# Where the big on-chip buffer begins: 192 bytes ahead of KV in a decode kernel that streams 170 MB

## The chip, the core and the metric

The kernel runs on one core of a Trainium2 chip. The metric is the device time of one execution in microseconds (us); before the change it is 402.7 us, the median of three runs (402.51 to 402.73).

## What is computed

One token goes through two branches whose results are added to it: an attention block with a cache of 65,536 positions, and a small mixer MLP. All data are bf16.

```python
def _A_ref(x, k_cache, v_cache, wq, wo):      # x [1,1,1024], k/v_cache [1,4,65536,128]
    q = heads(x @ wq)                          # 32 query heads of 128, 8 to a KV head
    scores = einsum("bhqd,bhkd->bhqk", q, k) * (128 ** -0.5)
    o = einsum("bhqk,bhkd->bhqd", softmax(scores), v)
    return merge(o) @ wo
def _B_ref(x, w1, w2, w3, w4):
    h = gelu(layernorm(x) @ w1)                # then a shift along the one position
    x1 = x + shifted(h) @ w2
    return x1 + gelu(layernorm(x1) @ w3) @ w4
xn = layernorm(A_x)
return A_x + _A_ref(xn, ...) + _B_ref(xn, ...)
```

With a sequence of length one the shift leaves only zeros, so the product with w2 is a product with zeros; the kernel still loads w2. Every cached key and value and every weight is read exactly once: 67 MB of keys, 67 MB of values and 36 MB of weights.

## The kernel before

**The buffer.** On-chip memory is laid out by the calls of `sb(...)` (L204), one tensor after another in the order of the calls, each rounded up to a multiple of 32 bytes of a partition. The last of them is `KV` (L257): 98,304 bf16 elements, 196,608 bytes in each of 128 partitions. In the program of before it begins at byte 31,552 of a partition, which is 123 x 256 + 64. All big transfers land in KV: keys in two slots of 32 KB a partition (`KOFF`, L258), values in two slots of 64 KB (`VOFF`), and the weights in the same slots before the first and after the last of the keys and values. `EPI` (L259) is a piece of the first value slot that holds small operands near the end. All offsets inside KV at which a transfer begins (L322, L333, L341, L621 to L627, L650, L651) are multiples of 256 bytes, so what KV's own first byte leaves after division by 256 is what every row of a transfer leaves.

**The transfers.** All of them but that of x are issued by SyncE (SP), from one queue. `issue_k(m)` (L325) loads 4 MB of keys: 128 rows, one to a partition, of 32 KB each. `issue_v(j)` (L335) loads 8 MB of values: 128 rows of 64 KB. wq and wo have rows of 64 KB, w3 of 56 KB, w4 comes in three pieces with rows of 32, 20 and 4 KB, w1 and w2 have rows of 16 KB (`load_rows`, L316, and `load_at`, L579). The 128 rows of a transfer are divided among the core's 16 DMA engines, 8 to each.

**The order.** wq goes first, then K0, V0, K1 (L323, L343 to L345). In the main loop (L584) step n handles 8,192 positions of one KV head; 32 steps in all. A key block serves two steps and a value block four. A slot is reloaded as soon as its last reader is done: `issue_k` after each odd step (L617), `issue_v` after each fourth (L619). So the queue receives K, K, V, K, K, V and so on: 16 key blocks and 8 value blocks, then w1, w2, w3 (L621 to L624), wo and w4 (L626, L627, L657).

**A step.** VectorE (DVE) transposes the keys of the slot in place, as 32-bit words, in four instructions (`Ttr`, L493); TensorE (PE) forms scores from them (`QK`, L503); VectorE takes maxima (L510); ScalarE (ACT) takes the exponential (L531); TensorE and VectorE transpose the result (L539, L541); TensorE multiplies with the values (`PV`, L549); ScalarE copies the product out (L557) and GpSimd (POOL) adds it to the running sum (L560, L562). After the loop come the products with w1, w2, w3, wo and w4 (L464, L665, L452), a cast (L699) and the transfer of the output (L700). The last weights to land are pieces of w4, read at L452.

Of the kernel before, what the change touches and what calls it, by code (L numbers as in the profile page):

```python
# [6 lines left out]
BF = mybir.dt.bfloat16  # L7
# [152 lines left out]
def _dma(q, chan, fn, reads=(), writes=(), partial=False):  # L160
    _deps(q, reads, writes)
    chan.n += 1
    ev = q.dma(fn, chan.sem, 16 * chan.n)
    _done(ev, reads, writes, partial)
    return ev


def bass_parallel_sum__gqa_block_cached__mixer_s_mlp__decode_kernel(
# [13 lines left out]
    P = 128  # L182
# [18 lines left out]
    with ExitStack() as es:  # L201
        E = es.enter_context

        def sb(name, shape, dt):  # L204
            return E(nc.sbuf_tensor(name, shape, dt))
# [48 lines left out]
        acc = sb("acc", [P, KT_D], F32)  # L254
        g_bf = sb("g_bf", [P, KT_D], BF)
        gh_bf = sb("gh_bf", [P, KT_F], BF)
        KV = sb("KV", [P, 98304], BF)  # L257
        KOFF, VOFF = (0, 16384), (32768, 65536)  # L258
        EPI = KV[:, 61440:65536].bitcast(F32)  # L259
        Dmat_f, Pmat_f = EPI[:, 1024:1152], EPI[:, 1152:1280]  # L260
# [29 lines left out]
        def chan(name):  # L290
            if name not in chans:
                chans[name] = _DmaChan(sem("d_" + name))
            return chans[name]
# [22 lines left out]
        def load_rows(dst, bufs, ch, w, r0, nrow):  # L316
            src = w.rearrange("(p r) n -> p (r n)", p=P)
            ncol = w.shape[1]
            _dma(q_sp, chan(ch), lambda e: e.dma_start(out=dst, in_=src[:, r0 * ncol:(r0 + nrow) * ncol]), writes=bufs)

        _dma(q_act, chan("x"), lambda e: e.dma_start(out=x_bf[:, :], in_=A_x[0, 0, :].rearrange("(p j) -> p j", p=P)), writes=[b_x])
        wq_sb = KV[:, VOFF[1]:VOFF[1] + 8 * HQD]  # L322
        load_rows(wq_sb, [b_V[1]], "wq", A_wq, 0, 8)  # L323

        def issue_k(m):  # L325
# [6 lines left out]
            sl = m % 2  # L332
            _dma(q_sp, chan("k%d" % sl), lambda e: e.dma_start(out=KV[:, KOFF[sl]:KOFF[sl] + 16384], in_=src), writes=b_K[sl] + b_T[sl])  # L333

        def issue_v(j):  # L335
# [4 lines left out]
            sl = j % 2  # L340
            _dma(q_sp, chan("v%d" % sl), lambda e: e.dma_start(out=KV[:, VOFF[sl]:VOFF[sl] + 32768], in_=src), writes=[b_V[sl]])  # L341

# [136 lines left out]

        KV32 = KV[:].bitcast(F32)  # L480
        kstep = KV[:].ap[0][0]
        pT_bf = pT_f[:].bitcast(BF).rearrange("p (q r two) -> p q r two", q=16, two=2)
# [253 lines left out]
```

## Time and profile before

| | before |
|---|---|
| median of three runs | 402.7 us |
| the profiled execution | 402.08 us |
| its span in the profile | 400.8 us, so 1.28 us lie around it |
| queue q1 (all big transfers) | 4,616 packets, 169.87 MB, 98.4% of 16 engines' span |
| mean rate over the span | 424 GB/s |
| VectorE, TensorE, GpSimd, ScalarE busy | 58%, 44%, 23%, 12% |
| granted TensorE clock, mean | 0.613 |

The profile is one execution. A busy share is the time in which an engine had an instruction, divided by the span; the DMA's share is the mean of the 16 DMA engines. The trace also holds a record of each DMA packet, with its queue, size, start and duration; here a packet is one row of a transfer (4 KB to 64 KB in one partition) or a 4-byte write that reports an engine's share of a transfer as done. A transfer counts as landed when all 16 engines have reported.

### The profile page before, as it was taken

The numbers are of one execution on the slowest core, as the hardware profiler recorded it, in microseconds if no ns is written. First come the engines' busy times: TensorE is split into PE (matmuls) and PEld (weight loads), VectorE is DVE, ScalarE is ACT, GpSimd is POOL, SyncE is SP. The second block draws the span as 40 slices with busy tenths as digits, with TensorE's granted clock in tenths as the row PEclk, the third lists the DMA queues.
The fourth block names the chain that finished last, engine by engine and source line by source line (L and its number), as shares of the span: only waits on it lengthen the run. The fifth ranks groups of instructions, "written<-read, shape, count | busy, mean of one in ns | idle before, by whom it ended". The sixth has DMA issues, their size and how long they took to land.

```text
span 400.8 us, 4663 instructions
## 1 busy us (share of the span) xinstructions
PE 175.5 (44%) x1504; PEld 54.0 (13%) x1504; DVE 232.5 (58%) x399; ACT 48.6 (12%) x132; POOL 91.5 (23%) x173
## 2 busy tenths in 40 slices
PE   0044244446254525443644464155426443454484
PEld 0022111111011101110111111011101110122132
DVE  0024756883688288738864886487657756643400
ACT  1000010211021101110111020111111120110000
POOL 6000013232135302230253021314332222250000
PEclk9997555655556656665555556656555555565888
DMA  9989999999999999999999998999999989999995
GB/s 392 445 366 471 414 419 419 491 395 422 461 420 422 422 451 464 392 419 458 432 419 419 484 438 386 422 461 438 405 432 484 432 379 425 482 414 413 437 410 210
DMA packets 4768, 169.98 MB, mean 424 GB/s; under 512 B 660, under 2 KB 664, under 8 KB 792
## 3 DMA queue, kind: packets, MB, share of 16 engines
q1 hardware_dynamic: 4616, 169.87, 98.4%
q8 instruction: 5, 0.08, 0.1%
q10 hardware_dynamic: 144, 0.00, 0.0%
q14 instruction: 3, 0.02, 0.0%
HBM read 169.87 MB, written 0.00 MB: 424 GB/s over the span
## 4 chain that ended last, share of the span: by engine, by line
DMA 57%; DVE 18%; PE 13%; issue 10%; ACT 1%; another core or an unknown queue 0%; DVEq 0%; POOL 0%; ACTq 0%; SPq 0%; POOLq 0%
DMA KV<-in_A_k_cache_dram 42%; DVE KV L493 13%; DMA KV<-in_B_w_dram 10%; PE S_ps L503 9%; DMA x_bf<-in_A_x_dram 6%; DVE mrow L510 2%; PE PT_ps L539 2%; PE OT_ps L549 1%; PE MM_ps L464 1%; ACT p_sb L531 1%; DVE pT_f L541 1%; PE MB_ps L516 1%; PE OUT_ps L452 0%; DVE Rm L511 0%; DVE Bst L520 0%
## 5 line engine op out<-in xcount | busy, mean ns | idle before, releaser
L493 DVE STREAM_TRANSPOSE KV<-KV 128x1024 f32<-128x1024 f32 x128 | 149.5, 1211 | 23.1 <-DMA KV<-in_A_k_cache_dram 23.1
L503 PE MATMUL S_ps<-KV,Ycur 128*32 128x512 bf16 x512 | 60.1, 617 | 83.5 <-DVE KV L493 83.2
L562 POOL TENSOR_TENSOR O_acc<-O_acc,tmpO 128x513 f32<-128x513 f32 x32 | 40.8, 1274 | 122.6 <-ACT tmpO L557 122.6
L549 PE MATMUL OT_ps<-KV,pT_f 128*32 128x512 bf16 x512 | 58.7, 609 | 19.5 <-DVE pT_f L541 18.7
L510 DVE TENSOR_REDUCE mrow<-S_ps 128x1 f32<-128x512 f32 x32 | 22.1, 691 | 39.6 <-PE S_ps L503 39.6
L531 ACT ACTIVATE p_sb<-S_ps,brun 128x512 bf16<-128x512 f32 x32 | 21.9, 686 | 136.3 <-DVE brun L529 119.5
L539 PE MATMUL PT_ps<-p_sb,permR 128*128 128x512 bf16 x32 | 17.6, 550 | 45.0 <-ACT p_sb L531 45.0
L557 ACT ACTIVATE tmpO<-OT_ps 128x512 f32<-128x512 f32 x32 | 19.2, 599 | 139.1 <-PE OT_ps L549 80.2
L503 PEld LDWEIGHTS S_ps<-KV,Ycur 128*32 128x32 bf16 x512 | 14.4, 125 | 124.4 <-DVE KV L493 95.4
L541 DVE STREAM_TRANSPOSE pT_f<-PT_ps 128x512 f32<-128x512 f32 x32 | 22.8, 713 | 13.3 <-PE PT_ps L539 12.3
L559 POOL TENSOR_TENSOR spare<-ff 128x1 f32<-128x1 f32 x32 | 6.2, 193 | 101.6 <-ACT ff L535 99.7
L549 PEld LDWEIGHTS OT_ps<-KV,pT_f 128*32 128x32 bf16 x512 | 15.7, 130 | 50.8 <-DVE pT_f L541 29.1
L560 POOL TENSOR_SCALAR O_acc<-O_acc,ff 128x514 f32<-128x514 f32 x32 | 22.4, 701 | 0.2 <-issue 0.2
L516 PE MATMUL MB_ps<-Rm,Lmat 128*128 128x16 bf16 x32 | 6.1, 192 | 25.5 <-DVE Rm L511 25.5
L520 DVE TENSOR_REDUCE Bst<-MB_ps 128x1 f32<-128x16 f32 x32 | 5.6, 174 | 14.2 <-PE MB_ps L516 14.2
L381 PE MATMUL MM_ps<-ln_s,ones_f 128*128 128x1 f32 x6 | 1.8, 362 | 27.1 <-DVE ln_s L380 27.1
L377 DVE CAST xT<-x_bf 128x8 f32<-128x8 bf16 x1 | 0.2, 172 | 21.4 <-DMA x_bf<-in_A_x_dram 21.4
L665 PE MATMUL S_ps<-KV,o_bf 128*1 128x512 bf16 x64 | 8.6, 437 | 5.6 <-DMA KV<-in_A_wo_dram 5.6
L516 PEld LDWEIGHTS MB_ps<-Rm,Lmat 128*128 128x128 bf16 x32 | 3.3, 102 | 53.3 <-DVE Rm L511 53.3
L393 POOL TENSOR_TENSOR ln_s<-ln_s,neghalf 128x1 f32<-128x1 f32 x3 | 1.7, 558 | 37.2 <-DVE ln_s L391 37.2
L539 PEld LDWEIGHTS PT_ps<-p_sb,permR 128*128 128x128 bf16 x32 | 3.2, 102 | 47.8 <-ACT p_sb L531 47.8
L691 DVE COPY KV<-S_ps 64x512 f32<-64x512 f32 x1 | 0.7, 682 | 11.5 <-PE S_ps L665 11.5
(112 smaller groups left out, 120.7 us busy)
## 6 DMA issues: line engine op xcount, KB each, us to landing
KV<-in_A_k_cache_dram SPq DMA_DIRECT2D x16, 4096.0 KB, 23.7
KV<-in_B_w_dram SPq DMA_DIRECT2D x1, 7168.0 KB, 33.2
KV<-in_B_w_dram SPq DMA_DIRECT2D x2, 2048.0 KB, 14.5
KV<-in_B_w_dram SPq DMA_DIRECT2D x1, 4096.0 KB, 35.4
KV<-in_B_w_dram SPq DMA_DIRECT2D x1, 2560.0 KB, 39.1
KV<-in_B_w_dram SPq DMA_DIRECT2D x1, 512.0 KB, 40.0
KV<-in_A_v_cache_dram SPq DMA_DIRECT2D x8, 36.2
x_bf<-in_A_x_dram ACTq DMA_DIRECT2D x1, 2.0 KB, 22.1
```

Source lines behind the costliest of these rows:

```text
L493: ev = q_dve.op(lambda e, c=c: e.transpose(out=KV32[:, c:c + 1024], in_=KV32[:, c:c + 1024]))
L503: fns.append(lambda e, we=we, cm=cm, mv=mv: e.matmul(S_ps[32 * cm:32 * cm + 32, :], Ycur[:, we, :, :].rearrange("p a g -> p (a g)"), mv, s ...
L510: _op(q_dve, lambda e: e.reduce_max(mrow[:, m:m + 1], S_ps[:, :], axis=AX.X), reads=[b_S], writes=[b_mrow[m]])
L516: _op(q_pe, lambda e: e.matmul(MB_ps[:, 0:16], Lmat[:, :], Rm[:, m, :], start=True, stop=True), reads=[b_R[m], b_const], writes=[b_MB])
L531: _op(q_act, lambda e: e.activation(p_sb[:, m, :], S_ps[:, :], ACTF.Exp, bias=brun[:, m:m + 1], scale=SCALE, accum_out=tmpO[:, cL:cL + 1]) ...
L539: _op(q_pe, lambda e: e.matmul(PT_ps[:, :], permR[:, :], p_sb[:, m, :], start=True, stop=True), reads=[b_p[m], b_const], writes=[b_PT])
L541: _op(q_dve, lambda e: e.transpose(out=pT_f[:, :], in_=PT_ps[:, :]), reads=[b_PT], writes=[b_pT])
L549: fns.append(lambda e, q=q, q4=q4: e.matmul(OT_ps[32 * q4:32 * q4 + 32, :], pT_bf[:, q, :, 1], KV[:, v0 + 512 * q:v0 + 512 * (q + 1)], sta ...
L557: _op(q_act, lambda e: e.activation(tmpO[:, 1:513], OT_ps[:, :], ACTF.Copy), reads=[b_OT], writes=[b_tmpO])
L560: b_Oacc.set_write(q_pool.op(lambda e: e.tensor_scalar(out=O_acc[:, :], in0=O_acc[:, :], scalar1=ff[:, m:m + 1], scalar2=0.0, op0=ALU.mult ...
L562: ev = q_pool.op(lambda e: e.tensor_tensor(out=O_acc[:, m:m + 513], in0=O_acc[:, m:m + 513], in1=tmpO[:, m:m + 513], op=ALU.add), tick=(s_ ...
L665: _grp(q_pe, [lambda e, lhs=lhs, rhs=rhs, jj=jj: e.matmul(S_ps[32 * jj:32 * jj + 1, :], lhs, rhs[:, 512 * jj:512 * jj + 512], start=False, ...
```

## The change

It sets aside one more tensor, of 96 bf16 elements (192 bytes) in each partition, just ahead of KV. Nothing reads or writes it. KV then begins at byte 31,744, which is 124 x 256. Sizes of transfers, their order, all instructions and all waits stay as they are; every operand that lies in KV is moved by 192 bytes.

```diff
         acc = sb("acc", [P, KT_D], F32)
         g_bf = sb("g_bf", [P, KT_D], BF)
         gh_bf = sb("gh_bf", [P, KT_F], BF)
+        sb("align", [P, 96], BF)
         KV = sb("KV", [P, 98304], BF)
         KOFF, VOFF = (0, 16384), (32768, 65536)
         EPI = KV[:, 61440:65536].bitcast(F32)
```

## The prediction

> **What bounds the kernel now.** I began with the page's totals and its 40 slices, then took the DMA queues, the chain of waits, SyncE's issues, a table of stretches, and last the single packet records.
>
> ```profile
> span 400.8 us, 4663 instructions
> ...
> PE 175.5 (44%) x1504; PEld 54.0 (13%) x1504; DVE 232.5 (58%) x399; ACT 48.6 (12%) x132; POOL 91.5 (23%) x173
> ...
> DMA  9989999999999999999999998999999989999995
> ...
> q1 hardware_dynamic: 4616, 169.87, 98.4%
> ```
>
> The reader is to see that no engine is busy for more than 58%, while the transfers are at nine tenths or more in all but four slices, the last of which is the tail.
>
> ```profile
> 100.00:140.00 40.00, 17.06 (x140) 4.54 (x136) 26.54 (x40) 6.36 (x17) 12.76 (x24) 0.59 1.00 432
> 140.00:180.00 40.00, 16.72 (x136) 4.43 (x136) 27.21 (x41) 5.76 (x16) 9.14 (x13) 0.63 1.00 433
> 220.00:260.00 40.00, 16.83 (x136) 4.51 (x136) 27.75 (x42) 5.77 (x16) 8.56 (x12) 0.59 1.00 433
> ```
>
> The last two columns of these stretches are the DMA share and GB/s: in the main loop the 16 DMA engines never rest. The third sum is VectorE's; it has 12 us to spare in 40.
>
> ```profile
> 116.62 16.70 SPq L333 DMA_DIRECT2D KV<-in_A_k_cache_dram  x2
> 133.36 0.43 SPq L341 DMA_DIRECT2D KV<-in_A_v_cache_dram  x1
> 155.42 16.07 SPq L333 DMA_DIRECT2D KV<-in_A_k_cache_dram  x2
> ```
>
> These are SyncE's issues. One round of the loop (two key blocks and one value block) is 155.42 - 116.62 = 38.80 us; over the five rounds to the key issue at 310.54 it is 38.78 us. A round moves 16.78 MB, so 432.6 GB/s. The second key issue of a round ends at 133.3 us; the records show the transfer ahead of it in the queue ending at 138.1 us on the first engine. So the queue is refilled about 4.8 us before it would run dry. (In the first round, about 3 us.)
>
> ```profile
> 116.62 23.77 DMA KV<-in_A_k_cache_dram
> ...
> 155.42 23.74 DMA KV<-in_A_k_cache_dram
> ...
> 357.65 39.11 DMA KV<-in_B_w_dram
> 396.75 0.04 issue
> 396.80 1.88 PE OUT_ps L452 x47
> 398.68 0.02 issue
> 398.70 0.42 DVE p_sb L699
> ```
>
> In the chain of waits each round is held by a key transfer that stands in the queue, and the end is the landing of w4, then 2.3 us of products and a cast, then the output. The time is therefore the pace of the DMA engines plus a fixed start (first packet at 1.8 us) and tail.
>
> **The price of one row.** A packet record is a row. Rows of 32 KB in KV have a median of 1,215 ns, those of 64 KB 2,420 ns. The difference, 32,768 bytes in 1,205 ns, is 27.19 GB/s an engine, 435 GB/s for 16. What is left of a row after its bytes is about 10 ns, whatever its size: rows of 4 KB take 160 ns (150.7 for the bytes), those of 16 KB 613 (602.6). By the round it is a little finer: each engine moves eight rows of each of the three transfers, 1,048,576 bytes, 38.56 us by that rate; measured 38.78; the rest, 0.22 to 0.23 us over 24 rows, is 9.6 ns a row, the report of each transfer included.
>
> KV receives 16 key blocks, 8 value blocks and 8 pieces of weights, 32 x 128 = 4,096 rows, so 256 to an engine. All fixed costs together are 256 x 9.6 = 2.45 us.
>
> **The change part by part.** It removes no instruction, adds none, moves none past another, and adds no wait; no queue gets a new order.
>
> *The bytes of a row.* Start offset cannot change the number of bytes, and a cost for every piece of a row that crosses a boundary would grow with the row. The rows show a cost that does not grow: ten nanoseconds at 4 KB and at 64 KB. So if the start at 64 past a multiple of 256 costs anything now, it is once per row and sits inside the 9.6 ns. This is the upper bound of the gain: 2.45 us, 0.61%.
>
> [...]
>
> *The fixed part of a row.* The trace has no long row into an aligned KV, so I bound it. Packets of other kinds: a 4-byte report takes 9 ns, and so does a 16-byte row of x, which goes to byte 18,336 (160 past a multiple of 256). If 9 ns is the floor of any packet, only 9.6 - 9 = 0.6 ns can go: 256 x 0.6 = 0.15 us. Instruction-code packets of 8 KB take 307 to 309 ns where undisturbed, 5.7 ns over their 301.3; if an aligned row were like them, 9.6 - 5.7 = 3.9 ns goes: 1.0 us. The long packet is nearer in kind to a row, the short ones are nearer in queue and memory; I take the middle, about 2.3 ns a row, **0.6 us**, and keep 0.15 to 1.0 us as the forecast's own range.
>
> [...]
>
> *Below nothing.* Rows of one size are not alike: most of 32 KB take 1,213 to 1,215 ns, but over a fifth take 1,220 to 1,222. If every row took the long form, against the round's mean of 1,214.4, it would cost 7.6 x 256 = 1.9 us.
>
> *The engines' operands.* 128 key transposes (L493, mean 1,211 ns), 512 products of scores and 512 with values read KV 192 bytes further on, in the same pattern. A gain here is worth nothing, since the transfers hold the round. A loss is covered by the 4.8 us with which the queue is ahead: 16 transposes a round could each be 0.3 us (25%) longer before the queue ran dry. Uncovered is only L452 in the tail, 1.88 us: a tenth more would be 0.2 us.
>
> *The extra tensor* is not written or read; no instruction, nothing.
>
> **The sum**, on the profiled execution: 402.08 - 0.6 = 401.5 us. The median of the runs shown lies 0.62 us above that execution, so the forecast is 402.7 - 0.6 = **402.1 us**, 0.15% less. What a measurement of this kernel can tell from no change is about 0.2%, 0.8 us. What is late next stays what it was: the transfers.
>
> **The rivals.**
>
> *Nothing happens*, because the fixed part of a row is the packet's own, or because KV's offset is not what the change says: 402.7 us, within 0.15 us. For it: the 9 ns of packets of 4, 16 and 88 bytes at whatever offset. Against: the 8 KB packets with less. Chance 0.17.
>
> *Most of the fixed part goes*, 1.0 to 2.45 us: 400.3 to 401.7 us. For it: each row is one packet, and its fixed part may hold a broken first and a broken last piece. Against: it would have to go below the price of every other packet in the trace. Chance 0.20.
>
> *Slower:* with the new start, rows take the long form of 1,222 ns. Its place is the DMA engines' write into KV; its price is up to 1.9 us, 404.6 us; from 3.1 ns more a row (0.8 us in all) it decides. For it: over a fifth of the rows already do, and the trace does not say why. Against: a start on a boundary has no more pieces than one off it. Chance 0.13.
>
> The forecast has the other 0.50.
>
> **How the numbers follow.** Faster by over 0.2%: the upper part of the forecast's own range, 0.8 to 1.0 us out of 0.15 to 1.0, about a quarter of 0.50, so 0.12, with the 0.20 of the second rival: 0.32. Slower by over 0.2%: of the 0.13, the part over 0.8 us, a little less than all if long rows come in bulk: 0.11. Within: 0.57. Range: below, it takes in gains up to 1.9 us of the second rival (400.8), leaving out some 0.08; above, up to 0.5 us of loss (403.2), leaving out about 0.11.
>
> **What would show it.** In the changed kernel's trace the round between key issues should be 24 x 2.3 ns = 0.055 us shorter, 38.72 to 38.73 us; 32 KB rows about 1,213 ns, 64 KB rows about 2,418; the difference of the two still 1,205 ns; the wait for w4 should end near 396.2 us. A round of 38.78 says nothing happened; 38.6 that most of the fixed part went; over 38.85 the slower rival. If the difference between the two row sizes changed, my bound of 2.45 us would be wrong, and so would it be if the loop turned out not to be held by the transfers.

## The result and the profile after

| | before | after |
|---|---|---|
| median of ten runs each | 402.75 us (402.42 to 403.01) | 401.61 us (400.83 to 401.92) |
| ratio after / before | | 0.9971, 95% interval 0.9961 to 0.9980 |
| the profiled execution, its span | 402.08, 400.8 us | 401.81, 400.6 us |
| queue q1: packets, share of 16 engines' span | 4,616, 98.4% | 4,616, 98.3% |
| 32 KB rows of KV: the commonest durations | 1,215 ns (961 of 2,176), 1,222 (371), 1,213 (363) | 1,213 ns (2,155 of 2,176) |
| 64 KB rows: the commonest durations | 2,420 ns (467 of 1,280), 2,418 (302), 2,427 (178) | 2,418 ns (1,242 of 1,280) |
| a round of the loop, on the engine that reports first | 38.780 us | 38.685 us |

The change makes the kernel faster by 1.14 us, 0.29% (0.20 to 0.39% by the interval). The last line of the table is taken from the packet records: the time between reports of successive value blocks, over five rounds.

Lines of the changed kernel are numbered one higher. Its main loop, in the same stretches as before (the last two columns are DMA share and GB/s), and SyncE's key issues at both ends of five rounds:

```profile
100.00:140.00 40.00, 16.82 (x146) 4.47 (x140) 26.71 (x40) 6.37 (x17) 12.53 (x24) 0.59 1.00 433
140.00:180.00 40.00, 16.64 (x134) 4.61 (x136) 27.44 (x41) 5.77 (x16) 9.29 (x13) 0.54 1.00 433
220.00:260.00 40.00, 15.76 (x134) 4.47 (x136) 27.81 (x43) 5.77 (x16) 8.57 (x12) 0.59 1.00 433
```

```profile
116.69 16.65 SPq L334 DMA_DIRECT2D KV<-in_A_k_cache_dram  x2
...
310.07 0.33 SPq L334 DMA_DIRECT2D KV<-in_A_k_cache_dram  x1
```

The loop is bound as it was: the DMA share is 1.00 in all three stretches, and VectorE is busy for 26.7 to 27.8 us of 40, where it was for 26.5 to 27.8. Five rounds take 310.07 - 116.69 = 193.38 us by the issues, 38.68 a round, where they took 38.78. A GB/s column with three digits hardly shows it; the quotient of two times that are 200 us apart does.

The end of the chain of waits after:

```profile
357.10 38.50 DMA KV<-in_B_w_dram
395.59 0.04 issue
395.64 2.76 PE OUT_ps L453 x36
398.39 0.02 issue
398.42 0.42 DVE p_sb L700
```

Here is the puzzle of this result. The products that wait for w4 begin at 395.64 us in place of 396.80, so the transfers won 1.16 us. Yet the cast begins only 0.28 us earlier (398.42 against 398.70), because the same 48 products took 2.76 us in place of 1.88. The stretch from 394 to 400 us says why, in the kernel before and then in the changed one (the first sum is TensorE's, the third column from the end its granted clock):

```profile
394.00:400.00 6.00, 1.84 (x48) 0.95 (x48) 0.42 (x1) 0.00 (x0) 0.00 (x0) 0.82 0.31 125
```

```profile
394.00:400.00 6.00, 2.73 (x48) 1.50 (x48) 0.42 (x1) 0.00 (x0) 0.00 (x0) 0.50 0.16 61
```

The clock of these rows is a mean over 6 us, of which the products fill only a part. The first microsecond of the products alone, before and after, is plainer:

```profile
396.80:397.80 1.00, 1.00 (x40) 0.84 (x40) 0.00 (x0) 0.00 (x0) 0.00 (x0) 1.00 0.05 20
```

```profile
395.64:396.64 1.00, 1.00 (x20) 0.65 (x24) 0.00 (x0) 0.00 (x0) 0.00 (x0) 0.50 0.12 49
```

In the profiled execution of before, TensorE did 40 of the 48 products in that microsecond, at a granted clock of 1.00; in that of after it did 20, at 0.50. So two questions were open: what in a row became cheaper, and whether the slower tail belongs to the new start.

### The profile page after: what moved, and what is told of

It is laid out like the page before. It is cut to its first block, busy times and chain, and to the rows that moved or that the text cites. A ratio compares the mean times of both kernels' runs of the same rounds, so it can differ in the third digit from the quotient of the medians.

```text
span 400.6 us, 4647 instructions
## 1 busy us (share of the span) xinstructions
PE 167.6 (42%) x1488; PEld 54.5 (14%) x1504; DVE 232.9 (58%) x399; ACT 48.6 (12%) x132; POOL 91.8 (23%) x173
## 3 DMA queue, kind: packets, MB, share of 16 engines
q1 hardware_dynamic: 4616, 169.87, 98.3%
## 4 chain that ended last, share of the span: by engine, by line
DMA 56%; DVE 21%; PE 12%; issue 9%; another core or an unknown queue 1%; DVEq 0%; POOL 0%; ACT 0%; SPq 0%; ACTq 0%; POOLq 0%
DMA KV<-in_A_k_cache_dram 41%; DVE KV L494 16%; DMA KV<-in_B_w_dram 10%; PE S_ps L504 9%; DMA x_bf<-in_A_x_dram 6%; DVE mrow L511 2%; PE OT_ps L550 1%; PE MM_ps L465 1%; PE OUT_ps L453 1%; DVE pT_f L542 1%; PE MB_ps L517 1%; DVE Bst L521 0%; DVE Rm L512 0%; DVE brun L530 0%
## 5 line engine op out<-in xcount | busy, mean ns | idle before, releaser
L494 DVE STREAM_TRANSPOSE KV<-KV 128x1024 f32<-128x1024 f32 x128 | 149.5, 1211 | 21.8 <-DMA KV<-in_A_k_cache_dram 21.8
L540 PE MATMUL PT_ps<-p_sb,permR 128*128 128x512 bf16 x16 | 8.6, 540 | 22.0 <-ACT p_sb L532 22.0
L534 DVE TENSOR_TENSOR dd<-brun 128x1 f32<-128x1 f32 x32 | 5.4, 170 | 3.6
```

What stands on the lines that cost most here:

```text
L494: ev = q_dve.op(lambda e, c=c: e.transpose(out=KV32[:, c:c + 1024], in_=KV32[:, c:c + 1024]))
L540: _op(q_pe, lambda e: e.matmul(PT_ps[:, :], permR[:, :], p_sb[:, m, :], start=True, stop=True), reads=[b_p[m], b_const], writes=[b_PT])
```

## The experiments

All ratios are against the kernel before, on the same chip.

**Which starts are cheap.** Theories: A, a row pays in proportion to the bytes between its start and the boundary of 256 below it; B, any start off a multiple of 256 costs the same, once per row; C, a smaller boundary will do. The edit is one number:

```diff
-        sb("align", [P, 96], BF)
+        sb("align", [P, 32], BF)     # e1: start at 128; [P, 80]: 224; [P, 112]: 32; [P, 224]: 0
         KV = sb("KV", [P, 98304], BF)
```

> KV begins 128 bytes past a multiple of 256 (64 bytes set aside). Theory A, a row pays for the bytes from the boundary below its start, in proportion: the 4.0 ns a row that the start at 64 costs against the start at 0 (round of 38.78 us against 38.68, 24 rows) become 8.0 ns, so the round is 38.88 us and the time 1.0 us over the kernel before, ratio 1.0025. Theory B, any start off a multiple of 256 costs the same 4 ns: round 38.78, ratio 1.000. Theory C, 128 is as good as 256: round 38.68, ratio 0.997.

> KV begins 224 past a multiple of 256 (160 bytes set aside). Theory A: 14 ns a row over the aligned start, round 39.02 us, time 2.6 us over the kernel before, ratio 1.0064. Theory B: round 38.78, ratio 1.000. Theory C: as B.

> KV begins 32 past a multiple of 256 (224 bytes set aside). Theory A: 2.0 ns a row over the aligned start, round 38.73 us, ratio 0.9987. Theory B: round 38.78, ratio 1.000. Theory C: as B.

> KV begins on the next multiple of 256 (448 bytes set aside, byte 32,000; the changed kernel's 31,744 is also a multiple of 1,024, this one is not one of 512). If 256 is what matters, the same as the changed kernel: round 38.68 us, ratio 0.997. If it takes a multiple of 512 or 1,024: round 38.78, ratio 1.000.

Two more starts followed, with one run each, since rounds had come out a little longer at 32 and 224:

> KV begins 192 past a multiple of 256, a multiple of 64 like the starts at 64 and 128. A theory that came from the runs so far: any start off 256 costs about 4 ns a row, and one that is off 64 as well about 1 ns more. Then the round is 38.78 us here. If the cost goes with how far the start is from a boundary, or 32 and 224 were dearer for another reason, it is another number, for example 38.80 or more.

> KV begins 96 past a multiple of 256, no multiple of 64, like the starts at 32 and 224, but not next to a boundary of 256. By the theory of 64: round 38.80 us. If nearness to a boundary made 32 and 224 dearer: 38.78.

Measured, with the round from the reports as above, and what a row costs over the aligned start, (round - 38.685) / 24:

| start past a multiple of 256 | round, us | ns a row more | median, ratio and interval |
|---|---|---|---|
| 0 (byte 31,744, after) | 38.685 | 0 | 401.61, 0.9971 (0.9961 to 0.9980) |
| 0 (byte 32,000, e4) | 38.688 | 0.1 | 401.62, 0.9977 (0.9968 to 0.9986) |
| 32 (e3) | 38.804 | 5.0 | 402.90, 1.0005 (0.9996 to 1.0014) |
| 64 (before) | 38.780 | 4.0 | 402.75 |
| 96 (e10) | 38.776 | 3.8 | 402.86 (one run) |
| 128 (e1) | 38.778 | 3.9 | 402.77, 1.0008 (0.9998 to 1.0017) |
| 192 (e9) | 38.779 | 3.9 | 402.75 (one run) |
| 224 (e2) | 38.804 | 5.0 | 402.98, 1.0007 (0.9998 to 1.0016) |

A falls: 128 is no dearer than 64, and 32 is dearer than 64. C falls too. B holds but for the 1 ns at 32 and 224, and 256 is enough: byte 32,000 is no multiple of 512 and does as well. The theory of 64 that I formed in between falls with e10: 96 is no multiple of 64 and costs no more than 64. What 32 and 224 have in common is that they lie 32 bytes from a boundary; why that costs 1 ns more was not found.

**Once per row, or with the bytes?** Key blocks in four transfers and value blocks in eight, all with rows of 8 KB, at the old start (e5) and on the boundary (e6):

```diff
+        PIECE = 4096
...
+        def in_pieces(ch, c0, src, n, bufs):
+            _deps(q_sp, [], bufs)
+            for c in range(0, n, PIECE):
+                ch.n += 1
+                ev = q_sp.dma(lambda e, c=c: e.dma_start(out=KV[:, c0 + c:c0 + c + PIECE], in_=src[:, c:c + PIECE]), ch.sem, 16 * ch.n)
+            _done(ev, [], bufs)
...
-            _dma(q_sp, chan("k%d" % sl), lambda e: e.dma_start(out=KV[:, KOFF[sl]:KOFF[sl] + 16384], in_=src), writes=b_K[sl] + b_T[sl])
+            in_pieces(chan("k%d" % sl), KOFF[sl], src, 16384, b_K[sl] + b_T[sl])
```

> Start at 64 as in the kernel before, but each key block comes in four and each value block in eight transfers with rows of 8 KB: 1,088 rows an engine in place of 256. If a fixed 9.6 ns a row is paid, 832 more rows cost 8.0 us: ratio 1.020, as long as SyncE's sixteen issues a round keep the queue filled. If the cost goes with the bytes and not with the rows, ratio 1.000.

> The same short rows with KV on a multiple of 256. If the start costs 4.0 ns once per row, 1,088 rows save 4.35 us against the short rows at 64, in place of 1.02 us with the long ones; against the kernel before 832 x 5.6 ns more and 256 x 4.0 ns less, 3.6 us, ratio 1.009. If what alignment saves goes with the bytes or with the number of rounds, 1.0 to 1.15 us against the short rows at 64.

Measured: e5 410.69 us, 1.0195 (1.0180 to 1.0210); e6 406.04 us, 1.0087 (1.0073 to 1.0100). Between the two lie 4.65 us where the long rows give 1.14. The queue's line, the same in both, then a stretch of the loop and the end of the chain in e5 and in e6:

```profile
q1 hardware_dynamic: 19592, 169.88, 99.1%
...
100.00:140.00 40.00, 17.92 (x148) 4.77 (x151) 26.61 (x40) 5.76 (x16) 12.24 (x24) 0.58 1.01 422
...
404.53 2.76 PE OUT_ps L461 x48
```

```profile
100.00:140.00 40.00, 17.00 (x135) 4.63 (x136) 26.90 (x40) 5.76 (x16) 12.04 (x23) 0.54 1.01 428
...
399.99 2.57 PE OUT_ps L462 x48
```

The bytes are the same and the DMA share stays full (1.01; a share over 1 means that records of successive rows overlap a little, as in the trace of before, where more than 16 rows are on record at once for 1.08 of the 38.4 us from 116.6 to 155.0), so the loss of rate, 433 to 422, is the cost of the added rows; the boundary gives 6 GB/s of it back. On the engine that reports its last row first, the four kernels end at 395.42 (long, 64), 394.43 (long, 0), 403.46 (short, 64) and 399.12 us (short, 0). So 832 more rows an engine cost 8.04 us at 64, 9.7 ns each, and 4.69 us at 0, 5.6 ns each; and 1,088 rows save 4.34 us, 4.0 ns each. The price goes with the rows: about 9.6 ns each at the old start, 5.6 ns on the boundary.

Two rivals are settled by the packet records. Transfers grew in the same proportion as rows (32 to 136, and 256 to 1,088 an engine), so the times alone could also mean a price per transfer. But then one row in eight of an engine would be longer, and in e5 most are: of 16,384 rows of 8 KB, 8,096 take 312 ns, 3,067 take 319 and only 1,541 take 309, which 16,372 take in e6. Nor is a collision with the engines' own use of KV needed: in the tail of before, from 393.0 to 396.7 us, VectorE is idle and TensorE busy for 0.16 us, and yet 27 of the 28 rows of 20 KB that begin after 393 us take 764 ns; in the changed kernel the ten that do take 761.

**Is the tail slower for the new start?** Of the two last pieces of w4, only the first row of each is multiplied; 10 of its 28 rows are left out.

```diff
-        out_rows(*w4_rows(1))
-        out_rows(*w4_rows(2), last=True)
+        out_rows(w4_rows(1)[0][:1], w4_rows(1)[1])
+        out_rows(w4_rows(2)[0][:1], w4_rows(2)[1], last=True)
```

> Start at 64 as before; of the two last pieces of w4 only the first row of each is multiplied (8 products in the tail in place of 48; 10 of 28 rows of w4 are left out of the result). The tail products take 1.84 us at a granted clock of 0.81 and 2.73 us at 0.50 in the two profiles; here about 0.4. Ratio about 0.994 to 0.996, and the runs' spread of 0.6 us shrinks if the tail's clock made it.

> The same short tail with KV on a multiple of 256. If the transfers give 1.02 to 1.1 us and the rest of the difference between executions is the clock in the tail, it is 1.0 to 1.1 us faster than the short tail at 64, ratio about 0.992 against the kernel before, and its runs lie closer together than the 1.1 us of the changed kernel's. If the tail itself is slower for the new start, the difference between the two short tails is larger than that between the full ones, near 1.9 us.

Measured: e7 401.81 us (401.59 to 402.00), ratio 0.9982 (0.9973 to 0.9991); e8 400.57 us (400.48 to 401.15, four of five up to 400.66), 0.9953 (0.9939 to 0.9967). e7 saved less than expected (I had 0.994 to 0.996), and so e8 missed its 0.992 too; its gain over e7 is a little more than the 1.0 to 1.1 us expected. The end of the chain in e7, then in e8:

```profile
357.70 40.20 DMA KV<-in_B_w_dram
...
397.94 0.41 PE OUT_ps L452 x3
```

```profile
357.04 39.57 DMA KV<-in_B_w_dram
...
396.66 0.41 PE OUT_ps L453 x4
```

With a tail of 0.41 us in both, the change is worth 401.81 - 400.57 = 1.24 us, as the waits say (397.94 - 396.66 = 1.28), and not 1.9. So the new start does not make the tail slower. Eight products are few, but the full tails say the same: in the profiled executions at 32, 96, 128 and 192 (e3, e10, e1, e9) the 48 products take 2.73 us, as they do on the boundary (after, e4), at a granted clock of 0.50 each time. What differs between the two profiles above is the clock, 1.00 against 0.50 in the first microsecond of the products. The reader sees too why e7 saved little: the wait that ends last is now that for the last two rows, at 397.94, and in the profiled execution of before 40 of the 48 products had been done in the 1.1 us before that. In that execution, which began its products at 1.00, the 48 took 1.84 us; at 0.50 (after) they took 2.73, so some 0.9 us more stick out behind the landings.

This probably explains the scatter of the runs too. In the twelve of the kernel before beside e11, times are 401.92, 402.06, 402.09 and then 402.62 to 403.29. The profiled execution, 402.08, was among the low ones, and the median is among the high ones. They are not two clean groups: beside e1 and e7 times of 402.24 to 402.60 occur as well, and a tail can lie between the two, as in e11, where the 48 products took 2.58 us at 0.60 in their first microsecond and 0.50 after it. The profiled executions of two kernels with the same transfers agree: e2 was taken at 402.13 us with the products in 1.89 us, e1 at 403.12 us with the products in 2.76. The clock is known for profiled executions alone, and none with long rows on the boundary and the full tail began its products at 1.00 (0.50 in after and e4, 0.60 in e11); that the fastest runs there (400.67 to 400.83) did is not shown.

**The changed kernel again, and a version without the exposed tail.** e12 keeps KV on the boundary and loads the w4 piece of ten rows as two, so that fewer products are left when the end comes:

```diff
-        w4_parts = [(0, 16, KOFF[1], b_K[1][0]), (16, 10, KOFF[0], _B()), (26, 2, KOFF[0] + 10 * D, _B())]
+        w4_parts = [(0, 16, KOFF[1], b_K[1][0]), (16, 6, KOFF[0], _B()), (22, 4, KOFF[0] + 6 * D, _B()), (26, 2, KOFF[0] + 10 * D, _B())]
...
-        out_rows(*w4_rows(2), last=True)
+        out_rows(*w4_rows(2))
+        out_rows(*w4_rows(3), last=True)
```

> The changed kernel once more, on the same chip as the next one. If its gain is the transfers' 1.0 to 1.1 us and what scatters is the clock in the tail, ratio 0.997 again, with executions near 400.8 us (full clock in the tail) and near 401.7 (half).

> KV on a multiple of 256, and the w4 piece of ten rows is loaded as two, of six and of four rows. The products then wait with 24 for the piece before last in place of 48 after the late landing (40 and 8). If the tail of 2.76 us at half clock is what is exposed, 24 products less take about 1.1 us less there, about 0.8 to 0.9 us after the wait for the last two rows; eight more rows an engine cost 8 x 5.6 ns, 0.05 us: about 400.8 us, 0.8 us under the changed kernel, ratio 0.995. If the landing of the last two rows sets the end, nothing, 0.997.

Measured: e11 401.58 us (400.70 to 401.77), 0.9971 (0.9961 to 0.9982), seven of eight runs at 401.4 to 401.8 and one at 400.70; e12 400.73 us (400.47 to 400.89), 0.9950 (0.9937 to 0.9964). The tail of e12, in order of time:

```profile
393.22 0.83 PE L453 MATMUL OUT_ps<-KV,gh_bf 128*1 128x256 bf16 x24 [1.18 <-DMA KV<-in_B_w_dram]
...
395.65 1.02 PE L453 MATMUL OUT_ps<-KV,gh_bf 128*1 128x256 bf16 x16 [1.60 <-DMA KV<-in_B_w_dram]
...
396.86 0.59 PE L453 MATMUL OUT_ps<-KV,gh_bf 128*1 128x256 bf16 x8 [0.19 <-DMA KV<-in_B_w_dram]
```

24 products run 2.4 us before the next piece is there, 16 before the last, and 8 remain. The version is faster than both kernels, by 0.85 us than the changed one, and its runs lie within 0.42 us.

## Why the prediction was right, and where it was off

The time lies in the stated range. Within it, the outcome was not the one held likeliest: a change of less than 0.2% had a chance of 0.57, a gain over 0.2%, which came, 0.32.

1. *What bounds the kernel:* right. The loop's pace is that of the DMA engines before and after (a DMA share of 1.00 in the stretches of both), and 832 more rows an engine showed at full size in the time (8.04 us in e5).
2. *The bytes of a row:* right. The difference of the two row sizes is still 2,418 - 1,213 = 1,205 ns. The cost is once per row; e5 and e6 show it with rows a quarter and an eighth as long.
3. *The fixed part, 9.6 ns a row:* right as a size (9.7 in e5). *What of it goes, 2.3 ns, 0.6 us:* this is the term that was mis-sized. It was 4.0 ns, 1.02 us. I took the middle between two rows of the trace; the 8 KB instruction packets were the right neighbour (309 ns for most undisturbed ones, and 309 for an aligned row of 8 KB in e6), and the short packets the wrong one. That the bound from this neighbour, 3.9 ns, fell so near is partly luck: it takes 307 ns, the least of the packets, and sets a record's length against the 9.6 ns of the pace. Records are about 2 ns longer than the pace: an aligned 8 KB row has 7.7 ns over its bytes by its record and 5.6 by the ends of the kernels. That a 4-byte packet takes 9 ns did not mean that a long row holds 9 ns that cannot go: on the boundary 5.6 ns a row were left.
4. *From the profiled execution to the median:* the sum took the 0.62 us between them as given. They probably go with the clock of the tail: the profiled execution began its products at 1.00, and most times are like those of the executions profiled at 0.50. The difference of the medians is not touched by it, but that of the two profiles is, 0.27 us in place of 1.1.
5. *The engines' operands at nothing:* right. The 128 transposes take 1,211 ns on average in both profiles, and the tail is not slower for the new start (e7, e8, and the full tails at 0.50).
6. *The rivals.* "Nothing happens" falls. "Slower" falls, and its argument was read backwards: the rows of 1,222 ns are themselves a mark of the start off the boundary, for 2,155 of 2,176 rows take 1,213 ns on it. "Most of the fixed part goes" began at 1.0 us and the forecast's own range ended there. The rows' 1.02 us stands on that border and the measured 1.14 us beyond it, in the rival's range, though less than half of the fixed part went (4.0 of 9.6 ns). Whether it holds a broken first and a broken last piece no run shows.
7. *The signs to look for:* a row of 1,213 and 2,418 ns came as stated. The round was 38.685 us where 38.72 to 38.73 was stated, the wait for w4 ended at 395.6 where 396.2 was.

What stays open: the last engine to finish gains 1.1 to 1.2 us (397.55 to 396.44 us; 397.44 to 396.24 in e7 and e8) and 256 rows at 4.0 ns are 1.02. The five 16 KB packets of instruction code in queue q8 are also shorter after (886 to 952 ns in place of 971 to 1,073), but whether they make up the rest was not tried. Why the clock of the tail differs between executions was not tried.

## What to carry to other kernels

Where transfers set the pace, look at the first byte of the buffer: rows that start on a multiple of 256 bytes saved about 4 ns each here, 0.3% of the time with rows of 32 to 64 KB and 1.1% with rows of 8 KB. Work such a cost out per row before deciding whether it is worth a line, and compare durations of equal rows in the packet records: a spread among them was the sign (1,215 ns for 961 of 2,176 rows, 1,222 for 371). When a gain that the waits show is missing from the span, compare the granted clock of the two tails before blaming the change.

## What the runs showed that I had not expected

- The cost of a start off the boundary does not depend on how far off it is, from 64 to 192 bytes (3.8 to 4.0 ns a row), and is 5.0 ns at 32 and at 224.
- On the boundary nearly all rows of a size take the same time to the nanosecond (2,155 of 2,176; all 256 rows of 16 KB take 611 ns).
- The same 48 products in the tail take 1.84 us or 2.73 us in two executions, as they begin at a granted clock of 1.00 or run at 0.50; the 0.9 us between them is not much less than the gain of 1.14 us.
